# Turning quarter 2 of the last batch row's g on TensorE, and grouping the w_out–phi products in pairs of strips, in a fused attention and two-MoE kernel

## The chip, the cores and the metric

The kernel runs on one core of one Trainium2 chip. The metric is device time in microseconds (us) of one execution; the time before is 518.12 us, the median of 3 runs (517.38 to 519.41).

## What is computed

The reference chains three blocks, all in float32. Sizes: b = 8 batch rows, 8 heads, 512 tokens, 32 state slots, head size 64, model width 512.

1. Attention between tokens x and slots, both ways: `xread = softmax(x·stateᵀ/8)·state` over the slots and `sread = softmax(state·xᵀ/8)·x` over the tokens, joined to 544 rows of 512 for each b, 4352 rows in all.
2. A feed-forward block: `h = x @ w_in` (512 by 2048), `g = h` where h ≥ 1, 0 where h ≤ −1, `(h+1)²/4` between, then `y = g @ w_out` (2048 by 512).
3. A soft mixture of 8 experts with 4 slots each: `logits = y @ phi` (512 by 32); a softmax of the logits over all 4352 rows mixes the rows into 32 slot inputs; each expert applies `max(s @ w1, 0) @ w2`; a softmax over the 32 slots mixes the slot outputs back into rows.

## The kernel before, in words

The rows are worked through as 9 steps: b = 0 to 7 are the 512 token rows of each batch row, b = 8 (B, "last") are the 256 rows of `sread` from all batch rows.

`y` is never formed. Since `y @ phi = g @ (w_out @ phi)`, the kernel first builds `wp = w_out @ phi`, and the mixed slot inputs are formed from g and only then multiplied by w_out.

**Staging of the weights (b = 0).** w_in and w_out are passed in a 64-bit form and are converted to float32 on DVE and ACT (`convert`, `piece`). The eight stage tiles of w_out go through `conv_wo(i)`, i = 8 to 15, two tiles to a group g. Each stage tile holds two pieces k. For each piece: convert it into `cw_w[k]`, a quarter of `acc` (L194); multiply it by phi into the 32-row strip k of the PSUM tile `wps` (L195); turn it with four TensorE transposes into `wtp` (L196 to 198); copy that to `wD` (L199). After the second stage tile of a group, `wD` is written to DRAM (L202), `wps` is copied to `wsb`, turned by eight small matmuls (L207), and copied into `wp` (L208). In the loop over m of b = 0 the stage tiles are popped at the places that `CFG["todo"]` gives (L816 to 818).

**The loop (L803 to 905).** For each b and each of 16 column blocks m, `hstep` computes a 128 by 512 block of h on TensorE (L445, for b = 8 L453), ACT, POOL and DVE make g of it (L465 to 501), and g is used twice: by `estep` for the logits (L554), and turned (tokens to partitions) for the product F with the weights of the softmax over the rows, `dN` (`smblock`, L622 to 641). Four blocks m make a quarter k.

**Two ways to turn g.** `by_pe(b, c)` (L514) says which. Where it is false, `tstep` turns each block on DVE in 32 by 32 pieces into a gD tile (L534); after the fourth block four DMAs on the SP queue write the gD tile to DRAM (`gdr`, L541), and one DMA reads it back in the right order into a nat tile (L543). Where it is true, `tquarter` (L518) makes 16 TensorE transposes in four PSUM tiles `gtp` of 128 by 512 (L523), each copied by ACT into the nat tile (L525). For b = 0 and b = 8 all quarters go by TensorE; for b = 7 those in `CFG["pe"]`, before that quarter 3 alone; all others go by DVE and DRAM. For b = 7 `gtp` comes from the PSUM pool X (`gtpX`), which has two buffers and is shared with F among others.

**What sets the order.** The framework's planner orders the instructions of each engine by a simulated timeline and by their order in the program. From b = 2 to b = 7 TensorE is taken out of that (L806, L808): it works in the order in which the program is written. `group` (L122) gives every matmul after its first a much higher priority, so that they follow the first at once. In the loop, `tstep` or `tquarter` for block m−1 stands behind `hstep(b, m)` (L867 to 872); so a quarter k of b = 7 that TensorE turns stands behind `hstep(7, 4k+4)`, and for k = 3 behind the first step of b = 8.

**DMA queues.** Nearly all DMAs are issued on SP's queue, in order; an issue that waits holds up those behind it. The loads of w1 and w2 (L724, `prefetch`) are issued on it as places in SBUF come free (`give`); a few go on POOL's queue. In the last b the SP queue holds, in order: the read-back of quarter 1, one weight load, the four writes of quarter 2, its read-back, and then 28 weight loads.

**After the loop** come the slot inputs SI (L931), w1 (L950), w2 (`slot_out`, L983) and the combination into the output (`combine`, L1008).

Of the kernel before, what the change touches and what calls it, by code (L numbers as in the profile page):

```python
# [14 lines left out]
PE = mybir.EngineType.PE  # L15


CFG = dict(hp=2000, att7=(3, 5, 6, 7, 8, 10), og=1, n3=1, n3m=12, wS=['DP', 'AD', 'AD', 'AD', 'AD', 'DP', 'AD', 'DD', 'AD', 'AD', 'AD', 'AD', 'AD', 'AD', 'AD', 'AD'], xsm=13, k0=5, rg=6, spg=0, att0=6, att=7, V0=(2, 6, 10), Vn=(0, 4, 10), Vx=12, wn='H', wsev='adad', conv=(1, 2, 3, 4, 12, 13, 19, 21, 24, 26, 28, 32, 36, 40, 44, 48, 52, 56, 60), todo=[1, 1, 1, 2, 0, 0, 0, 3, 0, 0, 2, 2, 1, 1, 0, 0], E0=2, E=1, sm=1, tqB=(5, 9, 13), GP=10, pe=(3,), psH=3, gtpX=(0, 7), tq0=(13, 15), keep=(2, 3, 4, 5), x2=(1, 1), natm=1, warm=14, bounce7=None, split=1, wt=4, so='sscscscscscscscc', smm=(1, 2, 3, 4, 5, 6, 9), tqv=(), tqvm=0, first='x', apath=2, f32c=1, place=1, attm=(3, 6, 7, 8, 9, 12), subPm=True, loDm=False, bounce=(0, 1, 2, 3), bq=('s', 's'), xq='s', nat=((1, 11), (2, 2), (2, 3), (2, 11), (3, 2), (3, 4), (3, 9), (4, 2), (4, 3), (4, 9), (5, 2), (5, 3), (5, 9), (6, 2), (6, 4), (6, 9)), subP=(), mulD=(0, 1), loD=(0, 1), qlag=0, gv0='SSSSSSSSSSSSSSSS', gv='EEESEEESEEESEEES', gvS='BBBBBBBBBBBBBBBB')


@with_exitstack
def kernel(
# [20 lines left out]
    def pool(name, bufs, **kw):  # L43
        return ctx.enter_context(tc.tile_pool(name=name, bufs=bufs, **kw))
# [6 lines left out]
    small = pool("small", 2)  # L51
    psH = pool("psH", CFG["psH"], space=PSUM)
    psE = pool("psE", 1, space=PSUM)
    psV = pool("psV", 1, space=PSUM)
    psX = pool("psX", 5 - CFG["psH"], space=PSUM)
    dram = pool("dram", 1, space=bass.MemoryType.DRAM)
# [6 lines left out]
    phi_t = const.tile([128, 4, 32], F32, name="phi_t")  # L63
# [18 lines left out]
    def slot(name, tag=None, dt=F32):  # L82
        return slots.tile([128, 2048], dt, name=name, tag=tag or name)
# [8 lines left out]

    v_s = [slot(f"v{c}", dt=F32R) if c or not CFG["f32c"] else None for c in range(2)]
    a_st = slot("ast", tag="a1")
# [22 lines left out]
    mm = nc.tensor.matmul  # L117
# [4 lines left out]
    def group(calls, after=()):  # L122

        first = mm(**calls[0])  # L124
        for i in after:
            tc.add_manual_dep(first.ins, i.ins.name, SYNC, reason="side by side")
        with tc.high_priority(CFG["hp"]):
            for c in calls[1:]:
                e = mm(**c)  # L129
                tc.add_manual_dep(e.ins, first.ins.name, ORDER, reason="side by side")  # L130

    def act(out, in_, func=ACTF.Copy, **kw):
        return nc.scalar.activation(out=out, in_=in_, func=func, **kw)  # L133
# [3 lines left out]
    cw_w = [acc[:, 512 * i:512 * i + 512] for i in range(4)]  # L137
# [3 lines left out]
    def stage_load(i):  # L141
        if i >= 16:
            return
        src = win[i // 2, :, 1024 * (i % 2):1024 * (i % 2) + 1024] if i < 8 else wout[i - 8]
        dma(out=stage[i].bitcast(U32), in_=src.bitcast(U32))
# [5 lines left out]
    def nxt(i):  # L151
        later = [j for j in range(i + 1, 16) if stage[j] is stage[i]]
        return later[0] if later else 16

    def convert(src, dst, tmp):

        w = src.bitcast(U32).rearrange("p (f w) -> p f w", w=2)
        lo, hi, d = w[:, :, 0], w[:, :, 1], dst.bitcast(U32)
        nc.vector.tensor_scalar(out=d, in0=hi, scalar1=0x07FFFFFF, scalar2=3,
                                op0=ALU.bitwise_and, op1=ALU.logical_shift_left)  # L160
        nc.vector.scalar_tensor_tensor(out=d, in0=hi, scalar=0xC0000000, in1=d,
                                       op0=ALU.bitwise_and, op1=ALU.bitwise_or)
        if tmp is None:
            nc.vector.scalar_tensor_tensor(out=d, in0=lo, scalar=29, in1=d,
                                           op0=ALU.logical_shift_right, op1=ALU.bitwise_or)
        else:
            t = tmp.bitcast(U32)

            act(tmp, lo, ACTF.Relu, scale=-2.0 ** -29, bias=seven)
            act(t, tmp, ACTF.Relu, scale=-1.0, bias=seven)  # L170
            nc.vector.tensor_tensor(out=d, in0=d, in1=t, op=ALU.bitwise_or)

    def piece(i, k, dst):
        rot["t"] += 1
        tmp = None if rot["t"] in CFG["conv"] else cw_t[rot["t"] % 3]
        convert(stage[i][:, 1024 * k:1024 * k + 1024], dst, tmp)

    def conv_win(i):
        c, h = divmod(i, 2)
        for k in range(2):  # L180
            piece(i, k, win_t[c][:, 2 * h + k, :])
        stage_load(nxt(i))

    wps, wD = {}, {}

    def conv_wo(i):

        g, h = divmod(i - 8, 2)
        if h == 0:
            wps[g] = psE.tile([128, 512], F32, tag="E", name="wps")  # L190
            wD[g] = rot_g.tile([128, 4, 512], F32, tag="g", name="wD")
        for k in range(2 * h, 2 * h + 2):
            w = cw_w[k]
            piece(i, k % 2, w)  # L194
            mm(out=wps[g][32 * k:32 * k + 32, :], lhsT=phi_t[:, k, :], rhs=w, start=True, stop=True)  # L195
            tp = psX.tile([128, 4, 128], F32, tag="X", name="wtp")  # L196
            for x in range(4):
                nc.tensor.transpose(tp[:, x, :], w[:, 128 * x:128 * x + 128], ident)  # L198
            act(wD[g][:, :, 128 * k:128 * k + 128], tp)  # L199
        stage_load(nxt(i))  # L200
        if h == 1:
            dma(out=wo32[g], in_=wD[g].rearrange("p x d -> p (x d)"))  # L202
            sb = rot_q.tile([128, 512], F32, tag="q", name="wsb")
            act(sb, wps[g])
            wpp = wps[g][:, 0:128].rearrange("p (x n) -> p x n", x=4)
            for x in range(4):
                mm(out=wpp[:, x, :], lhsT=sb[:, 128 * x:128 * x + 128], rhs=R4, start=True, stop=True)  # L207
            act(wp[:, 4 * g:4 * g + 4, :], wpp)  # L208

    def load_x(b):  # L210
        (dma if CFG["xq"] == "s" or b < 3 else nc.gpsimd.dma_start)(out=xs_s, in_=xs[b])

# [192 lines left out]
    wS = {}  # L405
# [390 lines left out]
    drain(v0)  # L796
    drain(a0)
    todo = [lambda i=i: conv_win(i) for i in range(2, 8)] + [lambda i=i: conv_wo(i) for i in range(8, 16)]

    sm = None  # L800
    vg = None
    order = ExitStack()
    for b in range(B + 1):  # L803
# [11 lines left out]
        for m in range(NM):  # L815
# [9 lines left out]
            if b > 0 and m % 4 == 0:  # L825
                k = 4 * b + m // 4 - 2
                if k >= 4 and (steady or m == 0 or b == 1 and m >= 8):
                    estep(k // 4, k % 4)
                    if k % 4 == 3:
                        sm = smblock(k // 4)  # L830
# [24 lines left out]
            if b == 1 and m == CFG["E0"]:  # L855
                for k in range(4):
                    estep(0, k)
                sm = smblock(0)
            if last and m % 4 == CFG["E"]:
                if m >= 4:  # L860
                    estep(b, m // 4 - 1)
                else:
                    estep(b - 1, 3)
                    sm = smblock(b - 1)
# [46 lines left out]
    sm = smblock(B)  # L911
# [17 lines left out]
    for i in range(4):  # L929
        for jj in range(4):  # L930
            mm(out=SI[32 * jj:32 * jj + 32, :], lhsT=PT[:, jj, 32 * i:32 * i + 32],  # L931
               rhs=where["wo", i][1][jj], start=(i == 0), stop=(i == 3))
# [13 lines left out]
    for i in range(16):  # L946
        e, hf = divmod(i, 2)
        place, w = where["w1", i]
        for kt in range(4):
            mm(out=h1[hf][32 * kt:32 * kt + 32, :], lhsT=XD[e // 4][:, kt, 32 * (e % 4):32 * (e % 4) + 32], rhs=w[kt],  # L950
               start=(e == 0), stop=(e == 7))
# [9 lines left out]
    so = [sot[:, 512 * i:512 * i + 512] for i in range(2)]  # L961
# [8 lines left out]
    for hf in range(2):  # L970
        s = run["tail"][:, 1536 * (1 - hf):1536 * (1 - hf) + 512]
# [114 lines left out]
```

## Time and profile before

| what | value |
|---|---|
| median of 3 runs | 518.12 us (517.38 to 519.41) |
| the profiled execution | 520.69 us |
| its span, first to last instruction | 518.5 us |
| PE busy | 462.9 us (89%) |
| DVE busy | 369.0 us (71%) |
| ACT busy | 313.4 us (60%) |
| POOL busy | 209.5 us (40%) |
| mean granted TensorE clock | 0.944 |
| DMA moved | 142.39 MB, mean 275 GB/s |

The profiled execution took 2.19 us more than its span, and 2.57 us more than the median. Engines: PE is TensorE's matmuls, PEld its weight loads, DVE VectorE, ACT ScalarE, POOL GpSimd, SP the engine that issues most DMAs (SPq is its queue). A float32 matmul shows as two records, and a transpose as one. An engine's idle time counts only where it lies on the chain that ends last.

### The profile page before, as it was taken

Reading aid. Unit: us, or ns where it says so; the run is one execution under the profiler, and the core shown is the slowest. Engines: PE = TensorE matmul, PEld = TensorE weight load, DVE = VectorE, ACT = ScalarE, POOL = GpSimd, SP = SyncE. Lnnn points to the kernel's source line nnn. Section 1 sums busy time; section 2 is a strip of 40 time slices with the busy share of each in tenths; the row PEclk is TensorE's granted clock in tenths of the full one; section 3 lists DMA queues with packets and bytes.
Section 4 is the critical chain, followed back from the end, with each engine's and each line's share of the span. In section 5 each row is a group of like instructions: output and inputs, shape, how many; then the busy total and the mean of one; then the engine's idle time right before and its main releaser. Section 6 shows DMA issues by size and latency. Waiting matters only on the chain.

```text
span 518.5 us, 9979 instructions
## 1 busy us (share of the span) xinstructions
PE 462.9 (89%) x3757; PEld 267.5 (52%) x3757; DVE 369.0 (71%) x768; ACT 313.4 (60%) x613; POOL 209.5 (40%) x211
## 2 busy tenths in 40 slices
PE   5382999999989999999998998999999769799994
PEld 2130465566545555555565455556457548335583
DVE  2999798869568879969968987985896745310370
ACT  0778997677667667767766866866656426211242
POOL 0000000045527776776776776877573100110041
PEclk9685999999999999999999999999999979989965
DMA  8998072546449797697596877789589898899998
GB/s 314 420 419 362 6 317 84 164 163 181 145 163 332 268 292 247 205 322 253 197 314 201 283 265 239 274 284 336 185 277 353 322 398 323 301 385 418 385 298 292
DMA packets 40127, 142.39 MB, mean 275 GB/s; under 512 B 3984, under 2 KB 12560, under 8 KB 27920
## 3 DMA queue, kind: packets, MB, share of 16 engines
q1 hardware_dynamic: 38400, 133.91, 72.5%
q0 software_dynamic: 1680, 7.87, 4.4%
q8 instruction: 29, 0.48, 0.4%
q14 instruction: 18, 0.15, 0.1%
HBM read 100.34 MB, written 41.42 MB: 273 GB/s over the span
## 4 chain that ended last, share of the span: by engine, by line
PE 62%; DVE 11%; DMA 7%; POOL 7%; issue 6%; ACT 5%; SPq 1%; ACTq 0%; POOLq 0%
PE h L445 24%; DMA gdr<-gD 5%; POOL v L393 4%; PE E L124 4%; PE V L124 4%; PE F L124 3%; PE h L950 3%; POOL c L475 3%; PE ops L129 3%; PE h L453 3%; PE wps L195 2%; DVE g L497 2%; ACT c L133 2%; PE gtp L523 2%; PE wtp L198 2%
## 5 line engine op out<-in xcount | busy, mean ns | idle before, releaser
L445 PE MATMUL h<-a,v 128*128 128x512 f32 x744 | 192.4, 403 | 7.1 <-DVE g L497 7.0
L445 PEld LDWEIGHTS h<-a,v 128*128 128x128 f32 x744 | 133.6, 188 | 71.2 <-DVE g L497 20.0
L475 POOL TENSOR_TENSOR c<-c 128x512 f32<-128x512 f32 x84 | 87.1, 1043 | 118.4 <-ACT c L133 117.7
L133 ACT ACTIVATE c<-h,half 128x512 f32<-128x512 f32 x128 | 87.9, 688 | 47.8 <-PE h L445 29.6
L497 DVE SCALAR_TENSOR_TENSOR g<-h,c 128x512 f32<-128x512 f32 x112 | 74.7, 671 | 36.3 <-POOL c L475 30.3
L393 POOL TENSOR_TENSOR v<-vc,v 128x512 fp32r<-128x512 f32 x48 | 61.9, 1290 | 49.6 <-ACT vc L133 49.4
L534 DVE STREAM_TRANSPOSE gD<-g 128x512 f32<-128x512 f32 x108 | 74.9, 700 | 1.8
L133 ACT ACTIVATE v<-V 128x512 fp32r<-128x512 f32 x62 | 37.1, 598 | 11.9 <-PE V L129 10.6
L124 PE MATMUL V<-win,st_t 64*32 64x512 f32 x64 | 35.9, 643 | 6.8 <-ACT att L133 5.5
L129 PE MATMUL V<-win,st_t 64*32 64x512 f32 x448 | 39.1, 636 | 0.0
L133 ACT ACTIVATE vc<-V 128x512 f32<-128x512 f32 x48 | 28.6, 596 | 15.0 <-POOL v L393 15.0
L124 PE MATMUL F<-nat,dN 128*32 128x512 f32 x54 | 26.6, 614 | 7.0 <-DMA nat<-gdr 6.6
L129 PE MATMUL E<-g,wp 128*32 128x512 f32 x168 | 29.6, 605 | 0.0
L124 PE MATMUL E<-g,wp 128*32 128x512 f32 x56 | 29.3, 605 | 0.0
L133 ACT ACTIVATE c<-c 128x512 f32<-128x512 f32 x44 | 27.8, 632 | 0.7
L129 PE MATMUL F<-nat,dN 128*32 128x512 f32 x162 | 26.8, 615 | 0.0
L453 PE MATMUL h<-XSh,v 128*128 128x256 f32 x128 | 26.1, 294 | 0.2 <-ACT nat L133 0.2
L641 DVE SCALAR_TENSOR_TENSOR acc<-acc,al,F 128x512 f32<-128x512 f32 x28 | 19.4, 724 | 7.3 <-PE F L129 7.3
L453 PEld LDWEIGHTS h<-XSh,v 128*128 128x128 f32 x128 | 20.7, 192 | 4.9 <-issue 1.7
L1036 POOL DMA_DIRECT2D out_dram<-o x16 | 7.9, 500 | 36.3 <-DVE o L1004 30.2
L129 PE MATMUL ops<-so,LC 32*128 32x256 f32 x160 | 20.6, 371 | 0.9 <-ACT o L133 0.8
L133 ACT ACTIVATE o<-ops 128x256 f32<-128x256 f32 x34 | 11.5, 381 | 15.8 <-PE ops L129 15.8
(238 smaller groups left out, 817.7 us busy)
## 6 DMA issues: line engine op xcount, KB each, us to landing
gdr<-gD SPq DMA_DIRECT2D x108, 256.0 KB, 6.8
nat<-gdr SPq DMA_DIRECT2D x27, 1024.0 KB, 6.2
w<-in_w_dram SPq DMA_DIRECT2D x24, 1024.0 KB, 10.7
xn<-in_xn_dram SPq DMA_DIRECT2D x8, 1024.0 KB, 8.6
out_dram<-o SPq DMA_DIRECT2D x16, 512.0 KB, 4.4
xs<-in_xs_dram SPq DMA_DIRECT2D x7, 1024.0 KB, 8.7
w<-in_w_dram POOLq DMA_DIRECT2D x5, 1024.0 KB, 8.9
wb<-in_win_dram SPq DMA_DIRECT2D x4, 1024.0 KB, 11.4
```

The source lines that it names most:

```text
L124: first = mm(**calls[0])
L129: e = mm(**c)
L133: return nc.scalar.activation(out=out, in_=in_, func=func, **kw)
L195: mm(out=wps[g][32 * k:32 * k + 32, :], lhsT=phi_t[:, k, :], rhs=w, start=True, stop=True)
L393: nc.gpsimd.tensor_tensor(out=lo[:, G, :], in0=vf, in1=hi[:, G, :], op=ALU.subtract)
L445: mm(out=h, lhsT=v[:, G, f], rhs=a[:, G, :], start=(k == 0), stop=(k == 5))
L453: mm(out=h, lhsT=w[:, j, :], rhs=x[:, j, :], start=(k == 0), stop=(k == 11))
L475: nc.gpsimd.tensor_tensor(out=c, in0=c, in1=c, op=ALU.mult)
L497: gI[b, m] = nc.vector.scalar_tensor_tensor(out=g, in0=h, scalar=1.0, in1=c, op0=ALU.max, op1=ALU.min)
L534: nc.vector.transpose(out=gd[:, :, :, m4, :].rearrange("p c a i -> p a c i"), in_=gT[b, m].rearrange("p (a c i) -> p a c i", a=4, i=32))
L641: nc.vector.scalar_tensor_tensor(out=a, in0=a, scalar=al, in1=F, op0=ALU.mult, op1=ALU.add)
L950: mm(out=h1[hf][32 * kt:32 * kt + 32, :], lhsT=XD[e // 4][:, kt, 32 * (e % 4):32 * (e % 4) + 32], rhs=w[kt], start=(e == 0), stop=(e == 7))
```

## The change

Two edits, independent of each other:

```
-CFG = dict(... pe=(3,), ...)
+CFG = dict(... pe=(2, 3), ...)
```

```
@@ conv_wo
         for k in range(2 * h, 2 * h + 2):
             w = cw_w[k]
             piece(i, k % 2, w)
-            mm(out=wps[g][32 * k:32 * k + 32, :], lhsT=phi_t[:, k, :], rhs=w, start=True, stop=True)
             tp = psX.tile([128, 4, 128], F32, tag="X", name="wtp")
             for x in range(4):
                 nc.tensor.transpose(tp[:, x, :], w[:, 128 * x:128 * x + 128], ident)
             act(wD[g][:, :, 128 * k:128 * k + 128], tp)
+        group([dict(out=wps[g][32 * k:32 * k + 32, :], lhsT=phi_t[:, k, :], rhs=cw_w[k], start=True, stop=True)
+               for k in range(2 * h, 2 * h + 2)])
         stage_load(nxt(i))
```

The first makes `by_pe(7, 2)` true: quarter 2 of b = 7 is turned by `tquarter(7, 2)`, behind `hstep(7, 12)`, into nat tile 2 in the plain layout (`natL`). Its four DVE transposes, four DRAM writes and one read-back fall away, and 16 transposes and four ACT copies come in. The second puts the two products of a stage tile with phi side by side, behind both pieces' transposes, as one group of two strips; the number of products stays 16.

## Rows read from the trace of the kernel before

**Rows 1.** The page, chain that ended last, share of the span by engine

```profile
PE 62%; DVE 11%; DMA 7%; POOL 7%; issue 6%; ACT 5%; SPq 1%; ACTq 0%; POOLq 0%
```

**Rows 2.** Chain that ended last, 355 to 425 us: start, duration (us), what

```profile
398.56 15.39 DMA gdr<-gD
...
414.08 4.84 DMA nat<-gdr
...
419.05 1.03 PE F L124
...
420.13 0.81 PE F L124
...
420.99 1.58 PE h L453 x6
422.57 0.59 PE F L124
...
423.17 0.42 PE F L124
...
423.60 1.50 PE h L453 x11
```

**Rows 3.** Timeline of PE, 380 to 425 us; in brackets the idle time before

```profile
387.06 4.47 PE L445 MATMUL h<-a,v 128*128 128x512 f32 x18
...
419.05 1.03 PE L124 MATMUL F<-nat,dN 128*32 128x512 f32 x1 [6.65 <-DMA nat<-gdr]
```

**Rows 4.** Windows by engine: busy (instructions), then granted clock, DMA share, GB/s

```profile
412.00:420.00 8.00, 1.35 (x12) 0.43 (x10) 1.72 (x4) 0.82 (x2) 0.00 (x0) 0.74 0.68 251
```

**Rows 5.** Chain that ended last, 50 to 112 us, then pieces of it

```profile
by line: PE h L445 36.4%; PE wps L195 20.1%; PE wtp L198 13.1%; PE V L124 7.4%; PE wps L207 5.5%; PE E L124 4.8%; PE h L436 4.1%; PE S L124 3.0%; PE gtp L523 2.4%; PE eTp L280 1.4%; PE sp L129 1.3%; PE V L129 0.6%; PE sp L124 0.3%; PE S L12
...
55.52 0.97 PE wps L195 x2
...
61.44 0.98 PE wps L195 x4
...
70.01 1.70 PE wps L195 x6
...
104.32 0.44 PE gtp L523 x4
```

**Rows 6.** Timeline of ACT, 375 to 425 us

```profile
386.57 0.69 ACT L133 ACTIVATE c<-h,half 128x512 f32<-128x512 f32 x1 [2.18 <-DVE g L497]
...
401.35 0.58 ACT L133 ACTIVATE gD<-gtp 128x512 f32<-128x512 f32 x1
```

**Rows 7.** Chain that ended last, 143 to 150 us

```profile
143.41 0.60 PE gtp L523 x4
...
149.51 0.55 PE F L124
```

**Rows 8.** Timeline of DVE, 375 to 425 us

```profile
389.02 0.69 DVE L497 SCALAR_TENSOR_TENSOR g<-h,c 128x512 f32<-128x512 f32 x1
```

**Rows 9.** Groups of DVE's instructions by line, 380 to 392 us

```profile
L534 DVE STREAM_TRANSPOSE gD<-g 128x512 f32<-128x512 f32 x4 | 2.7, 700 | 0.1
```

**Rows 10.** Windows, 65 to 91 us: length, then PE, PEld, DVE, ACT, POOL busy, clock, DMA

```profile
65.00:78.00 13.00, 13.00 (x77) 8.01 (x77) 13.00 (x32) 12.68 (x26) 0.00 (x0) 1.00 0.77 311
78.00:91.00 13.00, 13.00 (x74) 6.97 (x71) 11.20 (x23) 10.17 (x19) 0.00 (x0) 1.00 0.20 82
```

**Rows 11.** Who waited for whom, 52 to 108 us: us in total, times, longest

```profile
DVE acc L159 <- PE wtp L198: 2.9, 3, 1.1
```

**Rows 12.** SP's weight loads (line 724) from 410 us: duration, first and last issue

```profile
L724 SPq DMA_DIRECT2D w<-in_w_dram x28: 327/328/529, 414.5 to 473.6; - x28
```

**Rows 13.** DMA issues from 472 to 474 us: KB each, us to landing

```profile
w<-in_w_dram SPq DMA_DIRECT2D x1, 1024.0 KB, 16.9
```

**Rows 14.** Instructions on w: duration, first and last start

```profile
L124 PE MATMUL SO<-w,hTD x32: 379/379/403, 474.3 to 492.4; 128*32 128x256 f32 x32
```

**Rows 15.** DMA, 448 to 450 us

```profile
DMA packets 21, 0.16 MB, mean 78 GB/s; under 512 B 2, under 2 KB 2, under 8 KB 2
```

More of the change, by code (lines that the diff above doesn't have):

```diff
@@ L15 @@
 PE = mybir.EngineType.PE
-CFG = dict(hp=2000, att7=(3, 5, 6, 7, 8, 10), og=1, n3=1, n3m=12, wS=['DP', 'AD', 'AD', 'AD', 'AD', 'DP', 'AD', 'DD', 'AD', 'AD', 'AD', 'AD', 'AD', 'AD', 'AD', 'AD'], xsm=13, k0=5, rg=6, spg=0, att0=6, att=7, V0=(2, 6, 10), Vn=(0, 4, 10), Vx=12, wn='H', wsev='adad', conv=(1, 2, 3, 4, 12, 13, 19, 21, 24, 26, 28, 32, 36, 40, 44, 48, 52, 56, 60), todo=[1, 1, 1, 2, 0, 0, 0, 3, 0, 0, 2, 2, 1, 1, 0, 0], E0=2, E=1, sm=1, tqB=(5, 9, 13), GP=10, pe=(3,), psH=3, gtpX=(0, 7), tq0=(13, 15), keep=(2, 3, 4, 5), x2=(1, 1), natm=1, warm=14, bounce7=None, split=1, wt=4, so='sscscscscscscscc', smm=(1, 2, 3, 4, 5, 6, 9), tqv=(), tqvm=0, first='x', apath=2, f32c=1, place=1, attm=(3, 6, 7, 8, 9, 12), subPm=True, loDm=False, bounce=(0, 1, 2, 3), bq=('s', 's'), xq='s', nat=((1, 11), (2, 2), (2, 3), (2, 11), (3, 2), (3, 4), (3, 9), (4, 2), (4, 3), (4, 9), (5, 2), (5, 3), (5, 9), (6, 2), (6, 4), (6, 9)), subP=(), mulD=(0, 1), loD=(0, 1), qlag=0, gv0='SSSSSSSSSSSSSSSS', gv='EEESEEESEEESEEES', gvS='BBBBBBBBBBBBBBBB')
+CFG = dict(hp=2000, att7=(3, 5, 6, 7, 8, 10), og=1, n3=1, n3m=12, wS=['DP', 'AD', 'AD', 'AD', 'AD', 'DP', 'AD', 'DD', 'AD', 'AD', 'AD', 'AD', 'AD', 'AD', 'AD', 'AD'], xsm=13, k0=5, rg=6, spg=0, att0=6, att=7, V0=(2, 6, 10), Vn=(0, 4, 10), Vx=12, wn='H', wsev='adad', conv=(1, 2, 3, 4, 12, 13, 19, 21, 24, 26, 28, 32, 36, 40, 44, 48, 52, 56, 60), todo=[1, 1, 1, 2, 0, 0, 0, 3, 0, 0, 2, 2, 1, 1, 0, 0], E0=2, E=1, sm=1, tqB=(5, 9, 13), GP=10, pe=(2, 3), psH=3, gtpX=(0, 7), tq0=(13, 15), keep=(2, 3, 4, 5), x2=(1, 1), natm=1, warm=14, bounce7=None, split=1, wt=4, so='sscscscscscscscc', smm=(1, 2, 3, 4, 5, 6, 9), tqv=(), tqvm=0, first='x', apath=2, f32c=1, place=1, attm=(3, 6, 7, 8, 9, 12), subPm=True, loDm=False, bounce=(0, 1, 2, 3), bq=('s', 's'), xq='s', nat=((1, 11), (2, 2), (2, 3), (2, 11), (3, 2), (3, 4), (3, 9), (4, 2), (4, 3), (4, 9), (5, 2), (5, 3), (5, 9), (6, 2), (6, 4), (6, 9)), subP=(), mulD=(0, 1), loD=(0, 1), qlag=0, gv0='SSSSSSSSSSSSSSSS', gv='EEESEEESEEESEEES', gvS='BBBBBBBBBBBBBBBB')
 @with_exitstack
@@ L194, in conv_wo @@
             piece(i, k % 2, w)
-            mm(out=wps[g][32 * k:32 * k + 32, :], lhsT=phi_t[:, k, :], rhs=w, start=True, stop=True)
             tp = psX.tile([128, 4, 128], F32, tag="X", name="wtp")
@@ L199, in conv_wo @@
             act(wD[g][:, :, 128 * k:128 * k + 128], tp)
+        group([dict(out=wps[g][32 * k:32 * k + 32, :], lhsT=phi_t[:, k, :], rhs=cw_w[k], start=True, stop=True)
+               for k in range(2 * h, 2 * h + 2)])
         stage_load(nxt(i))
```

## The prediction

> **What bounds the kernel now.** The page's chain of work that ended last comes first: TensorE carries 62% of it, DMA 7% [rows 1]. So a change is worth what it takes from TensorE's own work or from a wait of TensorE, at the place where it acts. The two edits act in two places, 300 us apart.
>
> Quarter 2 of b = 7: the chain around 400 us shows it twice, a DMA from gD to DRAM of 15.39 us and its read-back of 4.84 us, and right behind them a product F at 419.05 [rows 2]. The timeline of PE says what that meant: 6.65 us in which TensorE had nothing to do, ended by that read-back [rows 3]. The window from 412 to 420 us holds 1.35 us of TensorE work, at a mean granted clock of 0.74 [rows 4]; what follows runs slowly at first. F's two passes start with 1.03 and 0.81 us, where the next F takes 0.59 and 0.42; six h matmuls take 1.58 us where eleven later ones take 1.50 [rows 2]. The granted clock has fallen towards the lower of its two levels, 1.2 GHz, behind the idle stretch.
>
> The staging of w_out (55 to 104 us): the chain from 50 to 112 us is TensorE throughout, with products `wps` at 20.1% of its 62 us, 12.46 us [rows 5]. TensorE is busy 13.00 of 13 us in the windows from 65 to 91 us [rows 10], so there its own work is the bound.
>
> **Edit 1: quarter 2 of b = 7 on TensorE (A).**
> *Removed from the path.* The wait, 6.65 us [rows 3]. And the slow start behind it: F 1.84 against 1.01 us in its two leading pieces, 0.83 us; six h matmuls 1.58 against 6/11 of 1.50 = 0.82, 0.76 us [rows 2]. Together 6.65 + 0.83 + 0.76 = 8.2 us. With quarter 2 in SBUF long before, TensorE finds F's input ready. What is late next I take to be nothing: quarter 3 comes by TensorE already, and its F follows at once at 422.57 [rows 2].
> *Added to the path.* 16 transposes. Four take 0.44 us on the chain [rows 5], so 1.8 us if nothing waits. They stand in TensorE's written order between h of block 12 and h of block 13, so what they wait for, TensorE waits for. Three h take 4.47 us from 387.06 [rows 3], so block 12's ends at about 388.5. The last g they need starts at 389.02 and ends at 389.71 [rows 8]; but DVE loses the transposes of quarter 2, four of 0.70 us [rows 9], of which two stand ahead of that g, so it should be there at about 388.4. The four PSUM tiles come from two buffers: the third tile waits for the first copy of 0.58 us [rows 6], the fourth for the second. TensorE leaves after 0.44 + 0.58 + 0.58 + 0.44 = 2.0 us, and 2.7 if one ACT instruction of 0.69 [rows 6] stands ahead of the first copy. I take 2.4. From below 1.8; from above 6.1 us, which the last part of a turned quarter of b = 0 took from 143.41 until F at 149.51, with other ACT work between the copies [rows 7]. It is nearest to the lower end: ACT stood idle for 2.18 us around this place [rows 6].
> *Beside the path.* The four ACT copies (2.3 us) lie in that idle time. DVE's relief of 2.8 us buys nothing more, since TensorE ran the three h behind without a break [rows 3]; if its cover goes, this is a gain. On the SP queue four writes and a read-back fall away, and with them the stretch in which the queue stood behind the 15.39 us DMA: 28 weight loads wait until 414.5 [rows 12], and the first of them will now go out some 17 us sooner, where places are free. They meet the read-back of quarter 1, which is ahead of them in the queue; 1 MB of writes and 1 MB of reads are gone from the same stretch. I cost this at nothing.
> *Sum of A:* 8.2 − 2.4 = 5.8 us faster, between 2.1 and 6.4.
>
> **Edit 2: groups of two strips (B).** One product alone takes 0.97 us; where the planner happened to put two strips side by side, both took 0.98, and three 1.70 [rows 5]. The 16 products stand now as nine alone, two pairs and one run of three: 9 × 0.98 + 2 × 0.98 + 1.70 = 12.5 us, which agrees with the 12.46. Afterwards: eight pairs, 8 × 0.98 = 7.8. TensorE saves 4.6 us. What can eat it: in the window from 65 to 78 us DVE is busy all of 13.00 us and ACT 12.68 [rows 10]; the run of three and one lone product lie there, so the 0.7 us saved there may only show as idle time. Behind 78 us DVE has 1.8 us idle in 13 [rows 10]. A second price: the pair is multiplied behind both pieces' transposes, so a buffer `cw_w` comes free later. DVE now waits three times for such a buffer, 2.9 us in all [rows 11]; were that doubled with no cover, B would bring 1.7. No row excludes that DVE and ACT set the pace at once, and then B brings 0; more than 4.6 none offers. I take 4.6 − 0.7 = 3.9, near the upper end, since TensorE, not DVE, is without idle time there.
>
> The Trainium skill (TensorE: Matmul & The Clock Gate, "Measured speedup vs the span model") speaks against a full factor of two: it has three column strips at 2.38 times one, 0.79 for each. By that figure, as an estimate, a pair would take 1.24 us and B would save 2.5 instead of 4.6. The pair's row here is the measurement that decides [rows 5].
>
> **Sum.** 5.8 + 3.9 = 9.7 us. The profiled execution took 520.69 us, so 511.0 on its own terms; it stands 2.57 above the median of the runs, 518.12, so the prediction is 508.4 us.
>
> **Rivals.**
> *1. DVE and ACT take over the staging, or the planner lays the pairs so that TensorE waits for them: B brings nothing.* For: the full DVE in the window from 65 to 78 us [rows 10]. Against: TensorE has no gap there. Then A alone: 518.1 − 5.8 = 512.3. It covers the case that the group isn't laid side by side.
> *2. The turn costs its upper end, 6.1 us,* because the copies stand behind other ACT work. A is then 2.1: 518.1 − 2.1 − 3.9 = 512.1. For: the row of b = 0 [rows 7]. Against: ACT's idle time.
> *3. The weights set the end.* The last of SP's weight loads goes out at 473.6 [rows 12] and lands 16.9 us later [rows 13], at 490.5; the last group of SO that may read it begins at 492.4 [rows 14]. That is 1.9 us of room. If these loads don't move with TensorE, A gives only 1.9: 518.1 − 1.9 − 3.9 = 512.3. Against: around 449 us the DMA engines moved 78 GB/s [rows 15], so they had caught up; they start afresh as places come free, and places come free by TensorE's work, which moves.
> *4. Slower.* Place: TensorE's written order between h of blocks 12 and 13. ACT works in order; a `c` that waits for its buffer blocks the copy behind it, and such a wait was 2.18 us [rows 6]. If each of the four tiles meets one: 4 × (0.44 + 0.58 + 2.18) = 12.8 us, against 8.2 gained: A costs 4.6. With B at 1.7 the kernel takes 521.0. It decides from a turn above 8.2 us plus what B brings, 2.5 us a tile. Against: few `c` are left there to be waited for.
>
> **Numbers.** Both edits as worked out: 0.60, 508.4. Rivals 1 to 3, one alone, near 512: 0.11, 0.09 and 0.08. Two of them together, near 516: 0.07. Rival 4: 0.05. Half a per cent is 2.6 us, about what a measurement of this kernel can tell from no change. So faster 0.60 + 0.11 + 0.09 + 0.08 = 0.88, same 0.07, slower 0.05. The range: at the lower end A at 6.4 and B at 4.6 give 507.1, and 1.6 more for DVE's relief, if it reaches TensorE, 505.5; at the upper end one rival and part of a second, 514.0.
>
> **What would show it.** In the profile after: no idle time of TensorE ended by a read-back at an F of nat tile 2, and no window near 0.7 of the clock there; `gtp` read from g with 32 transposes instead of 16; four fewer DVE transposes and DRAM writes, one fewer read-back; the four copies of quarter 2 in a stretch in which TensorE stands for no more than 2.7 us before h of block 13. For B: eight pieces of `wps` of four records and 0.98 us each, TensorE still without gaps from 55 to 104 us, and the first logits of b = 0 some 4 us earlier. Wrong would be: a new wait of TensorE for DVE or ACT between 55 and 107 us (rival 1), ACT waits among the four copies (rivals 2 and 4), or SO waiting for w (rival 3).

## The result, and the profile after

The changed kernel takes **513.44 us** (median; 512.22 to 517.13), where the kernel before took 520.42 (517.38 to 525.18) beside it: ratio 0.9879, 95% interval 0.9855 to 0.9902, some 6.3 us faster. Two later comparisons of the same pair gave 513.93 against 518.51 (0.9931, 0.9897 to 0.9965) and 513.72 against 519.15 (0.9953, 0.9905 to 1.0000). The medians are those of all runs, while the ratios leave out runs that lie more than 1.5% above the fastest of their set (in the last one 17 of the 29 of the kernel before), so a ratio is not the quotient of the medians beside it. Over all sets of runs in this document the kernel before has a median of 519.35 us in 98 runs, the change 513.55 in 40. So both edits together bring about 5.8 us, not 9.7, and the time is 5 us above the 508.4 forecast.

The profiled execution of the change took 517.07 us, one of its slower ones (span 514.9). The chain that ended last, by engine, holds TensorE with 59% (62% in [rows 1]) and DMA still with 7%:

```profile
PE 59%; DVE 11%; ACT 7%; POOL 7%; DMA 7%; issue 6%; SPq 1%; POOLq 0%; ACTq 0%
```

**Quarter 2 of b = 7.** Timeline of PE after, 384 to 394 and then 405 to 416 us; in brackets the idle time before and what ended it:

```profile
384.97 1.66 PE L446 MATMUL h<-a,v 128*128 128x512 f32 x6
386.46 1.28 PE L524 MATMUL gtp<-cst_t,g 128*128 128x128 f32 x8
...
388.67 1.09 PE L524 MATMUL gtp<-cst_t,g 128*128 128x128 f32 x8
389.52 4.37 PE L446 MATMUL h<-a,v 128*128 128x512 f32 x18
...
410.75 0.88 PE L124 MATMUL F<-nat,dN 128*32 128x512 f32 x1 [1.72 <-DMA nat<-gdr]
```

The turn stands where it was expected, in two halves of eight transposes with an E product between them, and no idle time at all. The 6.65 us of [rows 3] are gone. But there is another wait for a read-back, 1.72 us at 410.75: F of quarter 1. The chain from 374 to 412 us (start, duration, what) says what is behind it, quarter 0's and quarter 1's way through DRAM:

```profile
377.49 10.39 DMA gdr<-gD
...
390.17 14.21 DMA gdr<-gD
...
404.46 6.16 DMA nat<-gdr
```

**The staging.** Timeline of PE after, 55 to 104 us. A product alone is one record of L124 or L129 twice (x2); a pair is two records of each:

```profile
67.78 1.03 PE L124 MATMUL wps<-acc,phi_t 128*32 128x512 f32 x2
...
70.73 1.04 PE L129 MATMUL wps<-acc,phi_t 128*32 128x512 f32 x2
...
79.92 1.05 PE L124 MATMUL wps<-acc,phi_t 128*32 128x512 f32 x2
80.89 2.35 PE L446 MATMUL h<-a,v 128*128 128x512 f32 x9
83.17 1.04 PE L129 MATMUL wps<-acc,phi_t 128*32 128x512 f32 x2
...
87.09 0.62 PE L124 MATMUL wps<-acc,phi_t 128*32 128x512 f32 x1
87.09 0.62 PE L129 MATMUL wps<-acc,phi_t 128*32 128x512 f32 x1
```

At 87.09 a pair runs side by side, as wanted. At 79.92 the group's first product (L124) runs alone, then nine records of h, and at 83.17 its second (L129), alone again. The higher priority that `group` gives the second didn't hold the two together. The same happens to the groups that end at 70.73 and 98.33 (the first product of the former ran with the pair ahead of it, at 67.78: three in the time of one). Five pairs are whole and three groups are split, so there are ten pieces, not eight: 9.8 us, where before took 12.5.

```profile
65.00:78.00 13.00, 12.70 (x78) 8.09 (x78) 12.86 (x31) 12.59 (x27) 0.00 (x0) 1.00 0.73 263
...
91.00:104.00 13.00, 12.49 (x88) 7.29 (x77) 7.97 (x13) 9.09 (x21) 0.00 (x0) 1.00 0.55 203
```

In these windows (columns as in [rows 10]) TensorE now has gaps, 0.30 and 0.51 us; between 55 and 108 us it is idle for 0.8 us in all, where it had no gap before. That leaves 12.5 − 9.8 − 0.8 = 1.9 of the 4.6 us.

### The profile page after: what moved, and what is told of

The parts are those of the page before. It is cut to its first block, busy times and chain, and to the rows that moved or that the text cites. A ratio compares the mean times of both kernels' runs of the same rounds, so it can differ in the third digit from the quotient of the medians.

```text
span 514.9 us, 10000 instructions
## 1 busy us (share of the span) xinstructions
PE 465.1 (90%) x3773; PEld 272.6 (53%) x3773; DVE 366.3 (71%) x764; ACT 315.0 (61%) x617; POOL 209.5 (41%) x211
## 4 chain that ended last, share of the span: by engine, by line
PE 59%; DVE 11%; ACT 7%; POOL 7%; DMA 7%; issue 6%; SPq 1%; POOLq 0%; ACTq 0%
PE h L446 22%; DMA gdr<-gD 5%; POOL v L394 4%; PE E L124 4%; PE V L124 3%; PE h L454 3%; PE ops L129 3%; PE h L951 3%; PE F L124 3%; POOL c L476 3%; ACT c L133 3%; DVE g L498 2%; PE gtp L524 2%; PE SO L129 1%; PE SO L124 1%
## 5 line engine op out<-in xcount | busy, mean ns | idle before, releaser
L535 DVE STREAM_TRANSPOSE gD<-g 128x512 f32<-128x512 f32 x104 | 72.2, 700 | 1.7
L124 PE MATMUL V<-win,st_t 64*32 64x512 f32 x64 | 35.5, 636 | 6.8 <-ACT att L133 5.5
L129 PE MATMUL V<-win,st_t 64*32 64x512 f32 x448 | 38.6, 628 | 0.0
L129 PE MATMUL E<-g,wp 128*32 128x512 f32 x168 | 29.6, 605 | 0.0
L124 PE MATMUL E<-g,wp 128*32 128x512 f32 x56 | 29.3, 605 | 0.0
L124 PE MATMUL F<-nat,dN 128*32 128x512 f32 x54 | 26.6, 612 | 2.1 <-DMA nat<-gdr 1.7
L133 ACT ACTIVATE c<-c 128x512 f32<-128x512 f32 x44 | 28.1, 638 | 0.7
L129 PE MATMUL F<-nat,dN 128*32 128x512 f32 x162 | 26.9, 613 | 0.0
L129 PE MATMUL ops<-so,LC 32*128 32x256 f32 x160 | 21.5, 371 | 0.0
L133 ACT ACTIVATE o<-ops 128x256 f32<-128x256 f32 x34 | 12.5, 383 | 13.5 <-PE ops L129 13.4
```

The costliest lines, as they stand in the source:

```text
L535: nc.vector.transpose(out=gd[:, :, :, m4, :].rearrange("p c a i -> p a c i"), in_=gT[b, m].rearrange("p (a c i) -> p a c i", a=4, i=32))
```

## The experiments

Four lengths tell the versions apart; each is read from the timeline of PE of its profiled execution. *Front*: from the third stretch of h of b = 0, at 48.16 us in before, with which TensorE ends a wait of 9.53 us, to the attention scores S of b = 3; here B acts. *F*: from the attention's turn at 320 us to P, the first product on the finished acc behind the last F, where A acts. *To w1*: from P to the first w1 product. *Tail*: from there to the end of the span. (The expectations call that turn "eTp of b = 5"; it is the one for b = 7.)

| kernel | median us | ratio to before (95%) | profiled us | front | F | to w1 | tail |
|---|---|---|---|---|---|---|---|
| before | | | 520.69 | 107.2 | 103.0 | 27.8 | 62.3 |
| before_p1 | | | 517.78 | 106.2 | 101.4 | 27.8 | 62.3 |
| before_p2 | | | 522.09 | 106.2 | 107.6 | 27.8 | 60.4 |
| before_p3 | | | 520.99 | 107.2 | 105.6 | 27.8 | 60.5 |
| before_p4 | | | 527.74 | 107.2 | 111.9 | 27.8 | 60.9 |
| the change | 513.44 | 0.9879 (0.9855–0.9902) | 517.07 | 105.4 | 100.1 | 28.1 | 63.4 |
| after_again | 513.93 | 0.9931 (0.9897–0.9965) | 513.80 | 105.1 | 96.5 | 29.6 | 62.5 |
| after_3 | 513.72 | 0.9953 (0.9905–1.0000) | 512.26 | 105.0 | 96.6 | 28.1 | 62.8 |
| a_only | 514.46 | 0.9901 (0.9866–0.9937) | 514.50 | 107.0 | 96.6 | 28.1 | 62.9 |
| b_only | 517.46 | 0.9954 (0.9926–0.9983) | 516.73 | 105.6 | 102.6 | 27.8 | 60.7 |
| ab_hold | 512.82 | 0.9873 (0.9841–0.9905) | 512.23 | 105.1 | 96.6 | 28.1 | 62.4 |
| ab_hold_again | 513.78 | 0.9912 (0.9878–0.9946) | 514.12 | 105.1 | 96.6 | 29.7 | 62.9 |
| ab_hold_3 | 513.65 | 0.9953 (0.9921–0.9985) | 514.31 | 105.1 | 96.6 | 29.8 | 62.9 |
| ab_pairs | 518.64 | 0.9986 (0.9955–1.0017) | 519.59 | 103.0 | 96.6 | 29.4 | 64.9 |
| ab_hold_pairs_z | 515.26 | 0.9941 (0.9915–0.9967) | 515.54 | 103.1 | 96.6 | 27.8 | 63.1 |
| ab_q1 | 515.06 | 0.9937 (0.9911–0.9962) | 515.69 | 105.8 | 97.7 | 27.8 | 64.0 |
| ab_pairs_order | 511.54 | 0.9920 (0.9876–0.9964) | 511.34 | 103.5 | 96.6 | 27.8 | 62.9 |

Between front and F lie another 169.9 to 170.0 us in all but three: ab_pairs 175.6, ab_hold_pairs_z 174.9, ab_pairs_order 171.0. a_only, b_only, ab_hold and ab_pairs share one set of runs of before (520.44); after_again, ab_hold_again, ab_hold_pairs_z and ab_q1 another (518.51); after_3, ab_hold_3 and ab_pairs_order a third (519.15).

The front holds some noise of its own. The first 4 to 6 us of it, up to the first h on `a` and `v` (timeline of PE, 53.76 us in before), just ahead of the first product of the staging, lie at the slow clock in some executions and less so in others: from 47 to 55 us the mean granted clock is 0.56 in before and 0.73 in before_p1, and the fronts are 107.2 and 106.2 us. Counted from that h, the front takes 101.5 to 101.6 us in all six profiles without edit 2, 100.2 to 100.7 in the eight with it, and 98.1 to 98.5 in the three with all pairs whole (ab_pairs, ab_hold_pairs_z, ab_pairs_order).

### Each edit alone

a_only is the kernel before with edit 1, b_only with edit 2:

```
a_only:  -pe=(3,)   +pe=(2, 3)
b_only:  conv_wo as changed, pe=(3,)
```

> Only quarter 2 of b = 7 is turned by TensorE; the products with phi stand as before. Theory: the load of the eighth w1 tile (w1 7) moves ahead of quarter 0's DRAM writes on SP, these take about 10 us instead of 6, and F of quarter 1 waits for its read-back. Then the fourth h of b = 2 starts where it did (162.1 us, within 0.4) and the first w1 product comes 2.7 us earlier (at 453.5). Rival, the forecast's A without a new wait: 5.8 us earlier, at 450.4. Time: 2.7 to 4 us faster by the theory, 5.8 by the rival.

> Only the grouping; quarter 2 by DVE and DRAM as before. Theory: the planner lays some of the pairs apart and TensorE gets short gaps, so the fourth h of b = 2 starts 2.0 us earlier (160.1) and the first w1 product too (454.2); 2 us faster. Rival, the forecast's B: 3.9 us earlier at both places.

Measured: a_only 0.9901 of before, b_only 0.9954. In a_only the rival was right, with the first w1 product at 449.41. Edit 1 shortens F by 6.4 us, 103.0 to 96.6, and does so with no wait of F for quarter 1, though the SP queue holds the same DMAs in the same order as in the change: a weight load (for w1, piece 7, into the gD tile that quarter 2 no longer uses) stands ahead of quarter 0's writes in both. Edit 2 shortens the front by 1.6 us (mean of the five profiles of before and of a_only: 106.8; of three of the change, three of the held load below and b_only: 105.2), of which 1.2 us lie behind the first h on `a`; in b_only the theory was right, with the fourth h of b = 2 at 160.19 and the first w1 product at 453.85. F's wait stays where it was (b_only, timeline of PE):

```profile
415.48 1.03 PE L124 MATMUL F<-nat,dN 128*32 128x512 f32 x1 [5.04 <-DMA nat<-gdr]
```

So in F, A is as large as forecast, and B is the term that is too large. In the time of the whole kernel A is less: a_only's median lies 4.9 us below the 519.35 of all runs of before (6.0 below its own set), and the change lies 3.9 us below b_only.

### Is the new wait of quarter 1 the weight load's doing?

ab_hold is the change with that load ordered behind quarter 1's read-back on the SP queue:

```
-    back = lambda: q[...].dma_start(out=nat_of(b, c)...)
+    def back(): backs[b, c] = q[...].dma_start(out=nat_of(b, c)...)
...
     e = (... nc.sync).dma_start(out=t, in_=src[...])
+    if (kind, i) == ("w1", 7):
+        tc.add_manual_dep(e.ins, backs[B - 1, 1].ins.name, ORDER, ...)
```

> Both edits, with the load of w1 7 put behind the read-back of quarter 1 on SP's queue, in order of issue alone. Theory: quarter 0's writes take 6 to 7 us again instead of 10.4, quarter 1's read-back lands before 407, F of quarter 1 does not wait, and the first w1 product starts about 3 us earlier than with the change (448.3 instead of 451.5); time 2 to 3 us below the change, about 0.983 of before. Rival, the loads on POOL's queue alone make quarter 1 late: no difference to the change, 451.5.

> The changed kernel as it is, for a second profile beside other versions. Theory (the weight load of w1 7 in front of quarter 0's writes makes quarter 1's read-back late, in every execution): F of quarter 1 waits again 1 to 2.5 us for nat<-gdr near 410.8, the first w1 product stands near 451.5, and the time is 2.5 to 4 us above that of the version that holds the load back. Rival (the wait is only in some executions, and the profiled one was such a one): no wait of F or one under 0.5 us, first w1 product near 448.5, and both versions within 1 us of each other.

> The change with the load of w1 7 held behind quarter 1's read-back, a second time beside the change itself. Theory of the late read-back: 2.5 to 4 us below the change, first w1 product near 447.6 again. Rival (its time of 512.8 us is the change's own, and the held load buys nothing in most executions): within 1 us of the change.

> The held load alone a third time, beside the two others. Theory (the held load takes away only the rare executions in which the SP queue is some 5 us behind): median within 1 us of the change, and highest run below 517, where the change has about one run in five above 516. Rival (it makes no difference at all): as many runs above 516 as the change.

> The change a third time, beside the two others. Theory: median 513 to 514.5, some runs between 516 and 519; in the profile either no wait of F for a read-back, or one with the read-back of quarter 0 issued near 388 rather than 380. Rival (the wait of F belongs to the change in every execution): F waits over 1 us for nat<-gdr with the read-back of quarter 0 issued near 380.

Measured: ab_hold has no wait of F for a read-back and its first w1 product stands at 447.58, 3.9 us ahead of the first profile of the change. That looked like the theory. But the change itself has no such wait in its second and third profile either, its first w1 product is at 449.10 and 447.24, and the medians are 513.93 against 513.78 and 513.72 against 513.65. The held load buys nothing in the middle of the runs. The timeline of SP's queue shows why; read-backs and that load in the first profile of the change:

```profile
374.99 0.34 SPq L544 DMA_DIRECT2D nat<-gdr  x1
375.37 0.43 SPq L725 DMA_DIRECT2D w<-in_w_dram  x1
387.94 0.34 SPq L544 DMA_DIRECT2D nat<-gdr  x1
404.46 0.34 SPq L544 DMA_DIRECT2D nat<-gdr  x1
```

and in after_again:

```profile
369.33 0.34 SPq L544 DMA_DIRECT2D nat<-gdr  x1
369.71 0.43 SPq L725 DMA_DIRECT2D w<-in_w_dram  x1
380.22 0.34 SPq L544 DMA_DIRECT2D nat<-gdr  x1
393.88 0.34 SPq L544 DMA_DIRECT2D nat<-gdr  x1
```

In the first profile the queue is 5.7 us late before the load goes out, and loses 4.9 us more on the two quarters. In ab_hold the first two read-backs are 8.9 us apart (369.49 to 378.38), in after_again 10.9 (8.7 and 8.8 in the other two profiles of the held load, 11.0 in after_3): the load costs some 2 us, which F's slack covers in two of the change's three profiles. Of 40 runs of the change nine are above 516 us, of 26 of ab_hold two (516.2 and 516.3). These counts lean towards late executions being rarer with the held load, but they are too few to show it. The first profile is late at both quarters, so the load alone doesn't explain it; the last section has what else was in the way.

### How large is the wait of quarter 2 in the kernel before?

Four more profiles of the kernel before, nothing edited:

> The kernel before, for another profile. Theory (the wait of F for quarter 2's read-back differs from one execution to the next, since the SP queue gets through the quarters' writes and read-backs at different rates; the profiled 6.65 us is at the upper side): waits between 0 and 8 us, the execution's time going up and down with the wait and the slow clock behind it, mean of the profiles below 6.65. Rival (the wait is always near 6.65 us, and the spread of the times comes from elsewhere): all waits within 1 us of 6.65.

> As before_p1: waits of 0 to 8 us by theory, 5.7 to 7.7 us by the rival.

> As before_p1: waits of 0 to 8 us by theory, 5.7 to 7.7 us by the rival.

> As before_p1: waits of 0 to 8 us by theory, 5.7 to 7.7 us by the rival.

Measured (timeline of PE; p1's wait is 4.81 us at 415.94). before_p2:

```profile
410.04 1.03 PE L124 MATMUL F<-nat,dN 128*32 128x512 f32 x1 [2.12 <-DMA nat<-gdr]
...
421.45 1.03 PE L124 MATMUL F<-nat,dN 128*32 128x512 f32 x1 [6.53 <-DMA nat<-gdr]
```

before_p3:

```profile
420.34 1.03 PE L124 MATMUL F<-nat,dN 128*32 128x512 f32 x1 [8.50 <-DMA nat<-gdr]
```

before_p4:

```profile
414.19 1.03 PE L124 MATMUL F<-nat,dN 128*32 128x512 f32 x1 [5.35 <-DMA nat<-gdr]
...
426.39 1.03 PE L124 MATMUL F<-nat,dN 128*32 128x512 f32 x1 [6.79 <-DMA nat<-gdr]
```

The wait is no constant: 4.81 to 8.50 us for quarter 2, and in two of five executions quarter 1 waits as well, 2.12 and 5.35 us. So the "new" wait of quarter 1 in the first profile of the change isn't new; the kernel before has it too, when its queue is late. The theory's other half fell: the profiled 6.65 us was no upper value, as the mean of the five is 6.66 us for quarter 2 and 8.2 with quarter 1's. The times of the five executions rise in the order of their waits: 517.78, 520.69, 520.99, 522.09 and 527.74 us with 4.81, 6.65, 8.50, 8.65 and 12.14 us of both quarters together. Over these profiles F takes 101.4 to 111.9 us; in the versions that turn quarters 2 and 3 on TensorE it takes 96.5 to 96.6 in every profile but the first of the change. So edit 1 removes a spread of F as well as a length. In the times of the whole kernel that shows only in part: the standard deviation is 2.4 us over the 98 runs of before, 2.1 over the 40 of the change, 1.1 over the 26 of ab_hold, and 0.6 over a_only's six.

### A second quarter on TensorE

```
ab_q1:  -pe=(2, 3)   +pe=(1, 2, 3)
```

> The change with quarter 1 of b = 7 turned on TensorE as well. Theory (a turn costs TensorE some 2.1 us that nothing hides, and quarter 1's way through DRAM costs 1.7 us of waiting and about 1 us of slow clock only when the weight load is ahead of it): no wait of F for a read-back of quarter 1, first w1 product near 449.7, so 1.8 us before the change's 451.5 and 2.1 us behind the held load's 447.6; time 1.5 to 2.5 us above the version with the held load. Rival (a quarter on TensorE is worth 5.8 us each time, as quarter 2 was): first w1 product at 447 or earlier, time below the version with the held load.

Measured: 515.06, 1.3 us above ab_hold_again in the same set, where the theory had 1.5 to 2.5; the rival fell. F takes 97.7, 1.1 us more than with quarter 1 through DRAM and in time; each of its two turns has a gap now, 0.39 and 0.25 us (timeline of PE, the first):

```profile
378.55 1.15 PE L524 MATMUL gtp<-cst_t,g 128*128 128x128 f32 x8 [0.39 <-ACT nat L133]
```

So turning quarter 1 on TensorE costs more than it saves in an execution whose read-back is in time. The first w1 product came at 449.44, near the theory's 449.7, but partly for another reason: the front is 0.7 us longer than in the change, all of it in the stretch ahead of the staging.

### Where do the pairs' 4.6 us go?

ab_pairs gives the group of each stage tile a wait for the conversion of its second piece, so that its first product can't start alone:

```
-    piece(i, k % 2, w)
+    done = piece(i, k % 2, w)          # the last DVE instruction of the conversion
...
-    group([...])
+    group([...], [done])
```

> Both edits, and each group's first product waits until the second piece is converted too, so that no pair is laid apart. Theory: eight pieces of 0.98 us on TensorE instead of ten, and the fourth h of b = 2 starts 1 to 2 us earlier than with the change (158.1 to 159.1). Rival, DVE and ACT set the pace of the staging: it stays at 160.1 within 0.3, and TensorE's idle time between 55 and 104 us grows by what the pieces save.

Measured: all eight pairs are whole, some 0.99 us each, and the front falls to 103.0 us, 3.8 below the mean of before (4.2 below the profile that the prediction used; 3.3 from the first h on `a`). TensorE's idle time between 55 and 108 us is 0.84 us, about as in the change. So DVE and ACT don't set the pace: with whole pairs most of the 4.6 us is there. Yet the time is 518.64, worse than the change, since 5.6 us are lost between front and F, and the theory's own sign failed with it: the fourth h of b = 2 starts at 160.86, not at 158.1 to 159.1. Timeline of PE of ab_pairs at b = 2:

```profile
160.86 2.79 PE L446 MATMUL h<-a,v 128*128 128x512 f32 x6 [3.51 <-DVE g L498]
```

and DVE's timeline:

```profile
157.80 0.15 DVE L255 TENSOR_SCALAR rz<-sm 128x1 f32<-128x1 f32 x1 [0.67 <-ACT att L133]
...
158.32 0.69 DVE L290 TENSOR_REDUCE z<-att 128x16 f32<-128x512 f32 x1 [0.17 <-ACT att L133]
...
160.13 0.68 DVE L498 SCALAR_TENSOR_TENSOR g<-h,c 128x512 f32<-128x512 f32 x1
```

The planner, with the front shorter, lays the norms of the attention of b = 3 (rz, z) ahead of g of the first block of b = 2. They wait for ACT, g stands behind them, and TensorE stands behind g; the six records of h behind the wait take 2.79 us instead of 1.65. ab_hold_pairs_z adds the held load and orders z behind that g on DVE:

```
-    nc.vector.tensor_reduce(out=z1, in_=t3, ...)
+    e = nc.vector.tensor_reduce(out=z1, in_=t3, ...)
+    if b == 3: tc.add_manual_dep(e.ins, gI[2, 0].ins.name, ORDER, ...)
```

> Both repairs, and the norm of b = 3 ordered behind g of the first block of b = 2 on DVE. Theory (the pairs kept whole are worth 4.2 us at the start, and the earlier version with whole pairs lost them only by the 3.5 us in which TensorE waited for that g): attention 3 starts near 151, fourth h of b = 2 near 157.5, eTp of b = 5 near 320.5, first w1 product near 445.3, and the time 2 to 3 us below the version with the held load alone, near 510. Rival (the wait for DVE comes back at another place of b = 1 to 3, since DVE's other work is no earlier): fourth h of b = 2 at 159 or later, and the time within 1 us of the version with the held load, or above it.

Measured: 515.26; the rival was right. The wait came back with another releaser, as the timelines of PE, DVE and POOL say:

```profile
160.36 2.77 PE L448 MATMUL h<-a,v 128*128 128x512 f32 x6 [2.82 <-DVE g L500]
```

```profile
159.62 0.69 DVE L500 SCALAR_TENSOR_TENSOR g<-h,c 128x512 f32<-128x512 f32 x1 [1.23 <-POOL c L478]
```

```profile
156.53 2.05 POOL L271 TENSOR_TENSOR att<-att,m 128x512 f32<-128x512 f32 x2 [2.60 <-DVE nb L249]
158.54 2.04 POOL L478 TENSOR_TENSOR c<-c 128x512 f32<-128x512 f32 x2
```

DVE's g now waits for POOL's c, which stands behind the attention's subtraction, two of some 1.03 us. The attention had been laid ahead of b = 2's first block on every engine, not on DVE alone. ab_pairs_order holds it back on all three:

```
+    if b == 3:        # Exp on ACT behind c, the subtraction on POOL behind c * c,
+        tc.add_manual_dep(e.ins, cI[2, 0].ins.name, ORDER, ...)   # second rz and z on DVE behind g
+        tc.add_manual_dep(e.ins, pI[2, 0].ins.name, ORDER, ...)
+        tc.add_manual_dep(e.ins, gI[2, 0].ins.name, ORDER, ...)
```

> Held load, whole pairs, and now the attention of b = 3 ordered behind the first block of b = 2 on ACT (Exp behind c), POOL (subtraction behind c) and DVE (second rz and z behind g). Theory (the whole pairs' 4.2 us are lost at b = 2 only because the planner puts the attention's instructions ahead of c and g on ACT and POOL as well as on DVE): TensorE's wait before the fourth h of b = 2 falls from 2.8 us to 1.3 or less, no slow clock behind it, eTp of b = 5 near 321.5, first w1 product near 446.5 (448 with a stretch of slow clock around 440 to 455), and 1 to 2.5 us below the version with the held load alone. Rival (the front's gain is given back between b = 2 and b = 5 whatever stands there, as DVE's work per b is the bound): eTp at 323 or later and no gain over the held load.

Measured: **511.54**, 2.1 us below ab_hold_3 and 2.2 below the change in the same set, the lowest median of all versions (ten of its twelve runs take 512.8 us or less, against three of the change's twelve in that set). The theory was right. The wait at b = 2 is down to 0.47 us and the six records of h behind it are at 1.65:

```profile
158.09 1.65 PE L454 MATMUL h<-a,v 128*128 128x512 f32 x6 [0.47 <-DVE rz L257]
```

The first w1 product stands at 446.57, where the theory had 446.5. The front is 1.6 us shorter than in ab_hold_3; 1.0 of it is given back between front and F, and the turn at 320 us is 0.6 ahead. Of the 3.0 us between the two profiled executions the larger part lies in "to w1", 27.8 against 29.8: a stretch of slow clock that this profile lacks (last section). Against after_3, whose profile lacks it too, it is 0.9 us ahead (511.34 to 512.26). Whether its other runs lack that stretch no profile shows.

## Why the prediction was wrong where it was

**A, the wait removed: right in kind, and a draw from a spread.** The prediction took 6.65 + 0.83 + 0.76 − 2.4 = 5.8 us out of one profiled execution. Against that execution the stretch F became 6.4 us shorter. The turn measured 2.07 us (transposes from 386.46 to 387.68 and from 388.67 to 389.52) where 2.4 were taken; 8.24 − 2.07 = 6.2, so DVE's relief, costed at nothing, brings at most the 0.2 that is left. The rival of a turn at 6.1 us and the slower one both fell with this: no copy was waited for. What the prediction didn't see is that the wait is 4.8 to 8.5 us, with quarter 1's on top in some executions, so that a difference of two medians need not show the 5.8 of one profile.

**A, "What is late next I take to be nothing": wrong, in two places.** First the read-back of quarter 1, whose slack the prediction didn't measure: in a late execution of the change it costs 1.72 us and a slow stretch (F 100.1 against 96.6). The weight load that goes out early was costed at nothing; it takes some 2 us of that slack.

Secondly the tail. Where no slow stretch of clock falls into it ahead of the output, it takes 60.4 to 60.9 us without edit 1 (before_p2 to p4, b_only) and 62.4 to 62.9 with it (after_again, after_3, ab_hold three times, ab_pairs_order): 2 us of A's gain are given back. The sign is that of rival 3 (0.08), SO waiting for w, and no profile without edit 1 has it. Who waited for whom in after_3, 440 to 520 us:

```profile
PE SO L124 <- DMA w<-in_w_dram: 1.0, 2, 0.5
```

(In ab_pairs it is 2.0, and the tail 64.9.) But the mechanism is not the rival's. The loads did move with TensorE, as the prediction held; what changed is the planner's order of SO. Timeline of PE, the last group of SO in before_p2, in the first profile of the change and in after_3:

```profile
493.90 0.40 PE L124 MATMUL SO<-w,hTD 128*32 128x256 f32 x1
```

```profile
486.44 0.40 PE L124 MATMUL SO<-w,hTD 128*32 128x256 f32 x1
```

```profile
481.61 0.40 PE L124 MATMUL SO<-w,hTD 128*32 128x256 f32 x1 [0.51 <-DMA w<-in_w_dram]
```

Counted from SO's first product (475.89, 469.60 and 463.64 us in these three; 470.23 in b_only):

| us behind SO's start | before_p2 | b_only | the change, first profile | after_3 |
|---|---|---|---|---|
| last of SP's weight loads has landed | 17.9 | 17.9 | 16.3 | 18.0 |
| last group of SO starts | 18.0 | 17.9 | 16.8 | 18.0 |
| output's first product | 11.3 | 11.3 | 12.1 | 12.1 |
| end of the span | 44.0 | 44.3 | 45.3 | 46.4 |

The loads land as far behind SO's start in after_3 as in before_p2 and b_only. But with edit 1 the planner lays one more group of SO ahead of the output's first product, so that SO's last group is due 16.8 us behind SO's start, not 17.9, and has to wait for its weights. The 1.9 us of room that the prediction read [rows 14] belong to a profile in which w1 runs through a slow stretch of clock; so does the first profile of the change, where the loads land at 16.3 and nothing waits. In before_p2 and b_only there is next to no room. The wait is 1.0 of the 2 us. The rest probably comes from the output's later start: the first profile of the change has this order without the wait, and its end stands some 1 us further from SO's start than without edit 1. Why the planner changes its order the runs don't show, and a version with the old order of SO wasn't tried.

**B: 3.9 us forecast, 1.6 measured (1.2 without the stretch ahead of the staging); the step that failed is "eight pairs".** The arithmetic of a pair held: whole pairs took some 0.99 us ([rows 5] had 0.98), and with all eight whole the front is 3.3 to 4.2 us shorter, where the term was built on 4.6. What failed is that the change would make eight whole pairs. The group's first product has no reason to wait for the second piece's conversion, and the planner, which has h products ready, puts it to work at once; the higher priority that `group` gives the second is not enough to make it "follow the first at once". ab_pairs, which adds that wait and nothing else, makes all eight whole. The prediction's own row that showed the planner making pairs by chance [rows 5] was the hint that it also unmakes them; the case that the group "isn't laid side by side" stood in rival 1, which got 0.11 and priced it as B bringing nothing. Three split groups of eight cost more than half of what whole pairs save. The rival's other half, DVE and ACT as the bound, is refuted by ab_pairs. The price for buffers `cw_w` that the prediction doubled as a precaution did not show: TensorE's idle time is 0.8 us in the change and in ab_pairs.

The Trainium skill (TensorE: Matmul & The Clock Gate, "Measured speedup vs the span model") has three column strips at 2.38 times one, and by that a saving of 2.5 us was estimated, nearer to the 1.6 that came. It isn't the reason: the pairs run here at the full factor of two, and the three at 67.78 take 1.03 us. The span model of the same section, one product's time and some 4 ns for each further strip, agrees with these rows; the prediction left it out.

**The reference.** The forecast started from 518.12, the median of three runs; 98 runs have 519.35. Against 519.35 the forecast's 9.7 would have given 509.7. So of the 5.1 us by which the change's 513.55 lies above 508.4, 1.2 are the reference and 3.9 the saving that didn't come, 9.7 − 5.8.

**The sum.** 9.7 forecast; − 2.3 for B (3.9 − 1.6), − 2.0 for the tail, + 0.6 for A (6.4 − 5.8), − 0.3 in "to w1" (28.1 against 27.8) makes 5.7, and 5.8 us were measured between the medians over all runs. The agreement to 0.1 us is luck: it takes F from the one profile that the prediction used. With the mean F of the five profiles of before, 105.9, the same sum gives 8.6; but those five executions took 521.9 us on average, 2.5 more than the median of the runs, so they aren't typical either. What the sum shows is which terms were off, and which way: B and the tail, by some 2 us each. The prediction had rival 1 for the first, with all of B gone, and only the sign of rival 3 for the second.

## What to carry to other kernels

A group of instructions that is meant to run together has to depend on its last operand, or a planner that fills gaps will start the first and lay other work between; and holding the group together shifts the plan elsewhere, so look for the wait that comes next on every engine of that chain, not on the one named. A wait on a trip through DRAM, behind other traffic, is one draw from a spread: profile a kernel several times before taking its length as a term. And an edit can change the planner's order 100 us further on: before a stretch is taken as unchanged, compare its order, and what it comes to wait for, with the one before.

## What the runs showed of the hardware

One and the same quarter of b = 7, quarter 1 with its four writes of 256 KB and its read-back, takes from 11.5 us (before_p1, read-backs issued at 378.66 and 390.13) to 20.4 us (before_p4, 388.81 and 409.21) of the SP queue, with the same instructions on it. The traces show what else was under way. The DMA queues in these two stretches, before_p1 and before_p4; q1 carries the quarter, q0 the weight loads that POOL's queue issued:

```profile
q1 hardware_dynamic: 720, 2.10, 57.2%
q0 software_dynamic: 283, 1.27, 34.3%
```

```profile
q0 software_dynamic: 647, 4.36, 52.7%
q1 hardware_dynamic: 720, 2.10, 31.3%
```

The SP queue moves 2.10 MB in both (second number), POOL's 1.27 and 4.36. Over the five profiles of before the length of quarter 1 goes with the latter, and so does that of quarter 0 just ahead of it (timeline of SP and DMA queues, as above):

| | before_p1 | before | before_p3 | before_p2 | before_p4 |
|---|---|---|---|---|---|
| quarter 1, read-back to read-back, us | 11.5 | 12.9 | 13.8 | 16.6 | 20.4 |
| moved by POOL's queue meanwhile, MB | 1.27 | 1.97 | 2.81 | 3.55 | 4.36 |
| quarter 0, us | 9.0 | 9.2 | 10.1 | 10.5 | 10.9 |
| moved by POOL's queue meanwhile, MB | 0 | 0.08 | 0.55 | 0.75 | 0.87 |

A part of this goes the other way, since a longer stretch catches more of the loads. In the first profile of the change quarters 0 and 1 met 1.02 and 3.31 MB of them, in after_again 0.09 and 2.45. So the weight loads on POOL's queue, which no version changed, are the likely cause of a late read-back, next to the 2 us of the load on SP's. A version that holds them back wasn't tried, and why they go out at other times in other executions stays open.

The slow stretches of TensorE's clock also come in some executions of a program and not in others. The window from 435 to 440 us and the product P in it, behind short matmuls with gaps, in after_again and in after_3:

```profile
435.00:440.00 5.00, 4.12 (x29) 1.98 (x29) 2.41 (x12) 1.59 (x6) 0.39 (x1) 0.77 0.78 313
...
437.44 3.48 PE L618 MATMUL P<-nat,dN 128*32 128x512 f32 x16
```

```profile
435.00:440.00 5.00, 3.22 (x28) 1.54 (x28) 2.98 (x13) 1.26 (x6) 0.39 (x1) 1.00 0.72 287
...
437.11 1.92 PE L618 MATMUL P<-nat,dN 128*32 128x512 f32 x16
```

The mean granted clock is 0.77 against 1.00, so in after_again a part of the window lies at the lower of the two levels, 1.2 and 2.4 GHz. P takes 3.48 instead of 1.92 us and "to w1" 29.6 instead of 28.1: 1.5 us of difference with no instruction changed. Of the eleven profiles with edit 1 four have 29.4 us or more there; in before the like stands behind the first w1 product (the window from 455 to 460 us has 0.68 there). What decides whether it comes I can't tell from these runs.
